# Chunked retention with a GELU layer on one core: rows of q, k, v in 1 MB loads and transposes by DMA

## The chip, the cores and the metric

The kernel runs on one core of a Trainium2 chip. A core has a matrix engine (PE), a vector engine (DVE), an activation engine (ACT), a general engine (POOL) and a queue engine (SP) that only issues transfers; ACT and POOL issue transfers too. Each engine works through its own list in order and waits on semaphores. Sixteen DMA engines move the data. The metric is the device time of one execution, in microseconds.

## The reference

Two stages. The first is a retention recurrence over 768 steps, for 4 batches and 8 heads of 64; the second is a two-layer network with GELU over the 3072 rows that come out.

```python
# q, k, v: (4, 8, 768, 64)
gamma = 1.0 - 2.0 ** (-5.0 - np.arange(H))
for t in range(S):
    state = gamma[None, :, None, None] * state + einsum('bhd,bhe->bhde', k[:, :, t], v[:, :, t])
    y[:, :, t] = 1 / sqrt(64) * einsum('bhd,bhde->bhe', q[:, :, t], state)
x = y.transpose(0, 2, 1, 3).reshape(B * S, H * D)          # (3072, 512)
h = x @ w_in                                                # (3072, 2048)
g = 0.5 * h * (1.0 + tanh(c * (h + 0.044715 * h ** 3)))
return g @ w_out                                            # (3072, 512)
```

## The kernel before

The 768 steps are cut into six chunks (c = 0 to 5) of 128 steps, and inside a chunk the recurrence is written as products. For each batch b: A = k q^T within the chunk, masked with the decay (mm_A on PE, ev_A on DVE); y = state q + A v (mm_yc and mm_yi on PE, ev_Y); and the new state from k^T v (mm_s, ev_S). Then the network runs over the 512 rows of the chunk (4 batches of 128): moe1, 16 units of four matmuls of 512 columns, each with a GELU on ACT (two units with 256 columns in moe1_two for chunks 0 and 1), and the second product. For chunks 1 to 5 the second product is made in units_w by a scheme of seven products for a 2x2 block product in place of eight: seven groups of two units, eight matmuls of 256 columns a unit, whose left operands are sums of g that g_sums makes on POOL (DVE in the last chunk), 16 instructions in a chunk.

The order of work is written out by hand. `run(units, after)` goes through a list of units and puts other work behind a numbered unit: `8: [(load, 3)]` means behind the ninth. So the attention of chunk c + 1 and the loads and casts for chunk c + 2 lie between the units of the network for chunk c. For c = 2 to 5 units 0 to 15 are moe1 and 16 to 29 units_w.

q, k and v come as f32 with 64 elements (256 bytes) in a run. For PE they are cast to f16; A needs q and k transposed, heads in pairs: 128 partitions (two heads of 64) by 128 steps, four pairs to a batch, in the tile qkT. Before the change there are two ways to it:

- By PE (chunks 0, 1, and k of chunk 2): load1 (L100) brings a batch as rows, prep1 (L184) casts it, mm_T (L222) makes four transposes on PE for each of q and k into a PSUM bank, ev_T (L234) copies that to qkT.
- By blocks (q of chunks 2 to 5, k of chunks 3 to 5): load_blk (L106) makes 16 transfers of 64 KB, each of 512 runs of 128 bytes, which lay the 32x32 blocks at the right place; prep_blk (L201) casts a batch; one DVE transpose of 32x32 blocks (L238) for a batch ends it. The state needs k as rows too, so for chunks 3 to 5 k is loaded a second time as rows and cast by a prep1 of its own.

The kernel's buffers: k and v as rows have eight slots of one batch each; q has two tiles of a chunk each; the PSUM pool has two banks "h", two "o", four "att". The transfers of q, k, v from chunk 1 on are issued by SP, which also stores a few outputs; the stores of units_w go through POOL. A transfer takes one of eight semaphores in turn and waits for the transfer before it on the same one.

Lines that the change and the prediction touch: load (L117), prep1 (L184, cast at L180 and L182 by copy_on, multiplication at L193), mm_T (L222 to L232), ev_T (L234 to L245), moe1 and its GELU (L414, L416), g_sums (L476), units_w (L518) with its copies on ACT (L559, L565) and stores on POOL (L569), the schedule for chunk 1 (L734 to L769) and the loop over chunks 2 to 5 (L772 to L803).

Of the kernel before, what the change touches and what calls it, by code (L numbers as in the profile page):

```python
# [9 lines left out]
F16 = mybir.dt.float16  # L10
F32 = mybir.dt.float32
# [5 lines left out]
def kernel(  # L17
# [9 lines left out]
    nc = tc.nc  # L27
    B, H, S, Dh = q.shape
    C = 128
    NCk = S // C  # L30
    NHP = H // 2
# [26 lines left out]
    ld = ctx.enter_context(tc.tile_pool(name="ld", bufs=2 * B))  # L58
    pre = ctx.enter_context(tc.tile_pool(name="pre", bufs=2 * B))
    att = ctx.enter_context(tc.tile_pool(name="att", bufs=4))  # L60
# [13 lines left out]
    raw = {}  # L74
    srcs = {"q": q, "k": k, "v": v}

    BLK = {"q": (2, 3, 4, 5), "k": (3, 4, 5)}

    def ld_all(key):
        if key not in raw:
            raw[key] = ld.tile(
                [128, B * NHP, 4, 32],
                F32,
                tag=key[0],
                bufs=2 if key[0] == "q32" else 1,
                name=key[0],
            )
        return raw[key]  # L90

    def ld_tile(nm, c, b):
        if nm == "q":
            t = ld_all(("q32", c)).rearrange("p (b hp) a d -> p b (hp a d)", b=B)
            return t[:, b].rearrange("p (h d) -> p h d", h=H)
        if (nm, c, b) not in raw:
            raw[nm, c, b] = ld.tile([128, H, Dh], F32, tag=f"{nm}32", bufs=8, name=f"{nm}32")
        return raw[nm, c, b]

    def load1(eng, nm, c, b):  # L100
        eng.dma_start(  # L101
            out=ld_tile(nm, c, b),
            in_=srcs[nm][b, :, c * C:(c + 1) * C, :].rearrange("h p d -> p h d"),
        )

    def load_blk(nm, c):  # L106
        t = ld_all((nm + ("32" if nm == "q" else "T32"), c))
        src = srcs[nm].rearrange("b (hp j) s (dd d) -> j dd s (b hp) d", j=2, dd=2)
        for j in range(2):
            for dd in range(2):  # L110
                for a in range(4):
                    p0, t0 = (2 * j + dd) * 32, c * C + a * 32
                    nc.sync.dma_start(  # L113
                        out=t[p0:p0 + 32, :, a, :], in_=src[j, dd, t0:t0 + 32]
                    )

    def load(c):  # L117
        load_blk("q", c)
        if c in BLK["k"]:
            for b in range(B):  # L120
                load1(nc.sync, "v", c, b)
            load_blk("k", c)
            for b in range(B):
                load1(nc.sync, "k", c, b)
        else:
            for b in range(B):
                for nm in "kv":
                    load1(nc.sync, nm, c, b)

    def hold(nm, c, b, until):  # L130

# [18 lines left out]
        out=misc[:, 0:1], in_=zero[:, 0:1], func=AF.Gelu_apprx_tanh, scale=1.0  # L150
# [14 lines left out]
    for j in range(2):  # L165
        for hp in range(NHP):
            nc.vector.tensor_scalar(
                out=mask[:, j, hp],
# [4 lines left out]
            )  # L173

    h16 = {}
    blk16 = {}

    def copy_on(eng, out, in_):
        if eng is nc.scalar:
            eng.copy(out=out, in_=in_)  # L180
        else:
            eng.tensor_copy(out=out, in_=in_)  # L182
# [15 lines left out]
            )  # L198
        h16[nm, c, b] = t

    def prep_blk(eng, nm, c, b):  # L201
        key, tag = ("q32", "q16") if nm == "q" else ("kT32", "kT16")
        t = pre.tile([128, NHP * 4, 32], F16, tag=tag, bufs=6 if nm == "q" else B, name=tag)
        copy_on(
            eng, t, ld_all((key, c))[:, b * NHP:(b + 1) * NHP].rearrange("p hp a d -> p (hp a) d")
        )
        blk16[nm, c, b] = t

    def pair(t, hp):
        return t[:, 2 * hp:2 * hp + 2]  # L210

    qkT = {}
    a_sb = {}
    xT = {}
    pss = {}
# [3 lines left out]
    def bank(tag, dt=F32, shape=(128, NHP, 128), name="ps"):  # L219
        return psum.tile(list(shape), dt, tag=tag, bufs=BANKS[tag], name=name)  # L220

    def mm_T(c, b):  # L222
        parts = [(i, nm) for i, nm in enumerate("qk") if c not in BLK[nm]]
        if not parts:
            return
        ps = bank("att", F16, (128, 2, NHP, 128), "qkT_ps")
        for i, nm in parts:
            for hp in range(NHP):
                nc.tensor.transpose(  # L229
                    out=ps[:, i, hp], in_=pair(h16[nm, c, b], hp), identity=iden  # L230
                )
        pss["T", c, b] = ps  # L232

    def ev_T(c, b, eng=nc.vector):  # L234
        t = att.tile([128, 2, NHP, 128], F16, tag="qkT", name="qkT")
        for i, nm in enumerate("qk"):
            if c in BLK[nm]:
                nc.vector.transpose(  # L238
                    out=t[:, i].rearrange("p hp t -> p (hp t)"),
                    in_=blk16.pop((nm, c, b)).rearrange("p ha d -> p (ha d)"),  # L240
                )
        if ("T", c, b) in pss:
            i0 = sum(c in BLK[nm] for nm in "qk")
            copy_on(eng, t[:, i0:], pss.pop(("T", c, b))[:, i0:])
        qkT[c, b] = t  # L245

    def mm_A(c, b):
        t = qkT[c, b]
# [90 lines left out]
    def att_T(c, *bs):  # L339
        for b in bs:  # L340
            mm_T(c, b)
            ev_T(c, b)
# [73 lines left out]
    def moe1(c, fc):  # L416
        h_ps = bank("h", shape=(128, B * C), name="h_ps")
        moe1_mm(c, fc, h_ps, 0, B * C)
        gelu(g_tile(c, fc)[:, fc % 2], h_ps)
# [177 lines left out]
    def run(units, after):  # L597
        for i, u in enumerate(units):
            u()
            for f, *args in after.get(i, ()):  # L600
                f(*args)

    VE, AC, PO, SY = nc.vector, nc.scalar, nc.gpsimd, nc.sync
# [7 lines left out]
    prep1(PO, "k", 0, 0)  # L611
    prep1(AC, "v", 0, 0)
    mm_T(0, 0)
    ev_T(0, 0, AC)
    load1(AC, "k", 0, 3)
    prep1(VE, "q", 0, 1)
    prep1(PO, "k", 0, 1)
    spin(3)
    mm_A(0, 0)
    ev_A(0, 0)  # L620
    mm_T(0, 1)
    ev_T(0, 1, AC)
    prep1(AC, "v", 0, 1)
    spin(2)
# [73 lines left out]
    def preps(c, b):  # L698
# [44 lines left out]
            4: [(att_AY, 1, (3,), "o", 1, (), VE)],  # L743
            6: [(att_S, 1, 3)],
            7: [(g_sums, PO, 1, 4, 8, 0, 1)],
            8: [(prep_blk, AC, "q", 2, 0), (load, 3)],
            9: [(prep1, AC, "k", 2, 0)],
            10: [(att_T, 2, 0), (prep_blk, AC, "q", 2, 1)],
            11: [(prep1, AC, "k", 2, 1), (g_sums, PO, 1, 0, 4, 1, 2)],
            12: [(att_T, 2, 1)],  # L750
            14: [(att_AY, 1, (), "o", 2, (0, 1), None), (prep1, PO, "v", 2, 0), (prep1, PO, "v", 2, 1)],
            15: [(g_sums, PO, 1, 4, 8, 1, 2), (prep1, PO, "v", 2, 2), (prep1, PO, "v", 2, 3)],
        },
# [1 line left out]
    run(  # L755
        units_w(1),
        {
            0: [(prep_blk, AC, "q", 2, 2), (prep1, AC, "k", 2, 2)],
            1: [(att_T, 2, 2), (prep_blk, AC, "q", 2, 3), (prep1, AC, "k", 2, 3)],
            2: [(att_T, 2, 3)],  # L760
            4: [(att_AY, 2, (0, 1), "h", 2, (2, 3), AC)],
            7: [(att_S, 2, 0, 1)],
            9: [(att_AY, 2, (2, 3), "h", 2, (), AC), (att_S, 2, 2, 3)],
            10: [(prep_blk, AC, "q", 3, 0)] + [(prep1, PO, "v", 3, b) for b in range(B)],
            11: [(prep_blk, AC, "q", 3, 1)],
            12: [(prep_blk, AC, "q", 3, 2)],
            13: [(prep_blk, AC, "q", 3, 3)],
        },
    )  # L769

# [1 line left out]
    for c in range(2, NCk):  # L772
        n, m = c + 1, c + 2
        after = {} if n == NCk else {
            12: [(att_AY, n, (), "att", n, (0, 1), None)],
            15: [(att_T, n, 3)],
            16: [(prep1, AC, "k", n, 0), (prep1, AC, "k", n, 1)],
            17: [(prep1, AC, "k", n, 2), (prep1, AC, "k", n, 3)],
            19: [(att_AY, n, (0, 1), "h", n, (2, 3), VE)],
            22: [(att_S, n, 0, 1)],  # L780
            25: [(att_AY, n, (2, 3), "h", n, (), AC), (att_S, n, 2, 3)],
        }

        def more(at, *what):
            after[at] = after.get(at, []) + list(what)

        if n < NCk:
            for b in range(B - 1):
                if c == 2:
                    more((8, 9, 11)[b], (prep_blk, AC, "k", n, b))  # L790
                more(((9, 10, 13) if c == 2 else (6, 8, 13))[b], (att_T, n, b))
            if c == 2:
                more(13, (prep_blk, AC, "k", n, 3))
        for i in range(4):
            at = 4 * i + 3
            after[at] = [(g_sums, PO if n < NCk else VE, c, 2 * i, 2 * i + 2)] + after.get(at, [])
        if m < NCk:
            more(0, (load, m))
            for b in range(B):
                more((20, 21, 23, 24)[b], (prep_blk, AC, "q", m, b))  # L800
                more(24, (prep1, PO, "v", m, b))
                more(29, (prep_blk, PO, "k", m, b))
        run([(lambda fc=fc: moe1(c, fc)) for fc in range(NF)] + units_w(c), after)  # L803


# [28 lines left out]
```

## Time and profile before

| What | Value |
|---|---|
| Device time, median of three runs | 212.72 us |
| The runs | 211.48, 212.72, 212.92 us |
| Span of the profiled execution (its own device time is not listed apart) | 209.7 us |
| PE busy | 200.6 us |
| POOL busy | 115.4 us |
| Transfers on SP's queue (q1) | 108272 packets, 21.09 MB |
| Load of q, k, v: median from issue to landing | 4.0 to 4.7 us for 256 KB on SP, 2.7 and 2.8 us for 64 KB |

The span runs from the first to the last instruction of one profiled execution, and the device time holds some microseconds around it. A line of the profile names an engine, a line of the kernel, an operation, and the tile written and read with their shapes; busy time of matmuls is modelled and can overlap. The chain of waits is followed back from the last instruction: each piece is the work that the next one waited for. SPq, ACTq and POOLq are the transfers issued by those engines.

### The profile page before, as it was taken

How to read it: one execution, taken by the hardware profiler on the slowest of the kernel's cores; microseconds unless marked ns; L12 is line 12 of the kernel's file. 1: busy time of each engine (PE TensorE's matmuls, PEld its weight loads, DVE VectorE, ACT ScalarE, POOL GpSimd, SP SyncE). 2: the span in 40 equal slices, each digit the busy share in tenths (PEclk: the TensorE clock that was granted, in tenths of full speed). 3: DMA queues.
4: the chain of work that ended last, by engine and by line, in shares of the span. 5: the costliest groups of instructions: out<-in, count | busy, mean ns of one | idle time of the engine just before them, and what ended most of it. 6: DMA issues, size and time to landing. Idle time of an engine off the chain costs nothing.

```text
span 209.7 us, 4776 instructions
## 1 busy us (share of the span) xinstructions
PE 200.6 (96%) x1928; PEld 132.0 (63%) x1928; DVE 104.1 (50%) x213; ACT 101.9 (49%) x182; POOL 115.4 (55%) x120
## 2 busy tenths in 40 slices
PE   7789999999998999999999999999999999999992
PEld 3347644456786878844688744678644788545881
DVE  4445153478734649703857630867432784053430
ACT  2474563144458615168745266643365811566311
POOL 0596001133099999249998299997499980200000
PEclk9999999999999999999999999999999999999999
DMA  7999999998899798799798698796970000500004
GB/s 168 287 253 207 206 205 222 273 269 215 157 220 233 110 179 163 110 313 177 124 219 128 124 340 131 125 207 99 206 251 0 0 3 0 203 0 0 0 28 177
DMA packets 124438, 33.19 MB, mean 158 GB/s; under 512 B 117952, under 2 KB 122432, under 8 KB 124416
## 3 DMA queue, kind: packets, MB, share of 16 engines
q1 hardware_dynamic: 108272, 21.09, 50.3%
q0 software_dynamic: 5456, 8.65, 17.4%
q10 hardware_dynamic: 10688, 3.15, 6.4%
q8 instruction: 15, 0.25, 0.4%
q14 instruction: 7, 0.06, 0.1%
HBM read 30.78 MB, written 6.29 MB: 177 GB/s over the span
## 4 chain that ended last, share of the span: by engine, by line
PE 81%; SPq 6%; ACT 4%; DMA 4%; DVE 2%; issue 1%; ACTq 1%; DVEq 0%
PE h_ps L398 35%; PE o_ps L536 29%; SPq L113 5%; PE o_ps L432 5%; PE a_ps L252 3%; PE y_ps L289 3%; PE y_ps L276 2%; DMA iden<-rr_ident 2%; DMA v<-in_v_dram 2%; PE qkT_ps L229 2%; PE spin_ps L156 1%; SPq L101 1%; PE s_ps L313 1%; ACT g L414 1%; ACTq L101 1%
## 5 line engine op out<-in xcount | busy, mean ns | idle before, releaser
L398 PE MATMUL h_ps<-xT,w_in 128*128 128x512 f16 (+2 forms) x488 | 87.4, 334 | 0.5 <-ACT g L414 0.5
L414 ACT ACTIVATE g<-h_ps 128x512 f16<-128x512 f32 (+1 forms) x98 | 57.5, 589 | 33.9 <-PE h_ps L398 33.5
L398 PEld LDWEIGHTS <-w_in 128*128 128x128 f16 x488 | 45.3, 97 | 37.4 <-issue 2.8
L467 POOL TENSOR_TENSOR s_g<-g 128x512 f16<-128x512 f16 x32 | 36.9, 1152 | 9.4 <-ACT g L414 9.4
L265 DVE TENSOR_TENSOR a_sb<-a_ps,mask 128x512 f16<-128x512 f32 x48 | 30.1, 682 | 23.1 <-PE a_ps L252 23.1
L536 PEld LDWEIGHTS <-s_g 128*128 128x128 f16 x320 | 30.2, 98 | 4.3
L536 PE MATMUL o_ps<-t_w,s_g 128*128 128x256 f16 x240 | 27.8, 273 | 0.0
L536 PEld LDWEIGHTS <-g 128*128 128x128 f16 x240 | 23.4, 98 | 3.6
L467 POOL TENSOR_TENSOR s_g<-s_g,g 128x512 f16<-128x512 f16 x16 | 18.4, 1153 | 1.3
L536 PE MATMUL o_ps<-w_out,g 128*128 128x256 f16 x160 | 18.6, 273 | 0.0
L467 POOL TENSOR_TENSOR s_g<-g,s_g 128x512 f16<-128x512 f16 x16 | 18.5, 1153 | 0.0
L193 POOL TENSOR_TENSOR k<-k,cst 128x512 f16<-128x512 f32 x8 | 8.3, 1044 | 17.3 <-DMA k<-in_k_dram 17.3
L569 POOL DMA_DIRECT2D out_dram<-o_sb x8 | 5.9, 737 | 20.3 <-DVE o_sb L467 16.8
L193 POOL TENSOR_TENSOR v<-v,cst 128x512 f16<-128x512 f32 x16 | 16.2, 1044 | 0.0
L238 DVE STREAM_TRANSPOSE qkT<-kT 128x512 f16<-128x512 f16 x12 | 8.1, 678 | 15.0 <-ACT kT L180 9.5
L565 ACT COPY o_sb<-o_ps 128x512 f32<-128x512 f32 (+1 forms) x5 | 2.7, 543 | 25.1 <-PE o_ps L536 25.1
L432 PE MATMUL o_ps<-w_out,g 128*128 128x512 f16 x64 | 14.8, 380 | 0.0
L305 DVE TENSOR_TENSOR xT<-y_ps,dec 128x512 f16<-128x512 f32 x16 | 10.3, 686 | 4.5 <-PE y_ps L289 4.5
L238 DVE STREAM_TRANSPOSE qkT<-q 128x512 f16<-128x512 f16 x16 | 11.0, 690 | 2.6 <-ACT q L180 2.5
L559 ACT COPY s_u<-o_ps 128x512 f32<-128x512 f32 (+1 forms) x6 | 3.1, 514 | 17.6 <-issue 9.9
L330 DVE SCALAR_TENSOR_TENSOR st<-st,cst,s_ps 128x128 f16<-128x128 f16 (+1 forms) x40 | 10.1, 313 | 2.0 <-PE s_ps L313 2.0
L156 PE MATMUL spin_ps<-zero 128*128 128x512 f16 x32 | 9.4, 429 | 1.2 <-DVE zero L148 1.2
(55 smaller groups left out, 185.3 us busy)
## 6 DMA issues: line engine op xcount, KB each, us to landing
k<-in_k_dram SPq DMA_DIRECT2D x22, 256.0 KB, 4.7
v<-in_v_dram SPq DMA_DIRECT2D x18, 256.0 KB, 4.0
q<-in_q_dram SPq DMA_DIRECT2D x64, 64.0 KB, 2.8
out_dram<-o_sb POOLq DMA_DIRECT2D x8, 512.0 KB, 5.2
kT<-in_k_dram SPq DMA_DIRECT2D x48, 64.0 KB, 2.7
w_in<-in_moe_w_in_dram POOLq DMA_DIRECT2D x4, 512.0 KB, 9.3
w_out<-in_moe_w_out_dram POOLq DMA_DIRECT2D x4, 512.0 KB, 14.7
v<-in_v_dram ACTq DMA_DIRECT2D x6, 256.0 KB, 5.5
```

The lines of the kernel that those rows point to most:

```text
L113: nc.sync.dma_start(out=t[p0:p0 + 32, :, a, :], in_=src[j, dd, t0:t0 + 32])
L156: nc.tensor.matmul(out=ps, lhsT=zero[:, 0:128], rhs=zero, start=True, stop=True)
L193: eng.tensor_tensor(out=t, in0=src, in1=cst[:, col:col + H].unsqueeze(2).broadcast_to([128, H, Dh]), op=ALU.mult,)
L238: nc.vector.transpose(out=t[:, i].rearrange("p hp t -> p (hp t)"), in_=blk16.pop((nm, c, b)).rearrange("p ha d -> p (ha d)"),)
L265: nc.vector.tensor_tensor(out=s, in0=ps[j], in1=mask[:, j], op=ALU.mult)
L305: nc.vector.tensor_tensor(out=x, in0=ps, in1=dec, op=ALU.mult)
L330: nc.vector.scalar_tensor_tensor(out=t[:, :, hp], in0=t[:, :, hp], scalar=cst[:, OG + hp:OG + hp + 1], in1=s_ps[:, :, hp], op0=ALU.mult, o ...
L398: nc.tensor.matmul(out=out, lhsT=w_in_sb[wi][:, kc, wr * 128:(wr + 1) * 128], rhs=xT[c][:, kc, t0:t1], start=(kc == 0), stop=(kc == NHP - ...
L414: nc.scalar.activation(out=out, in_=in_, func=AF.Gelu_apprx_tanh, scale=1.0)
L432: nc.tensor.matmul(out=ps[:, n0:n1], lhsT=g_sb[c, fc // 8][:, fc % 8, b * C:(b + 1) * C], rhs=w_out_sb[fc // (NF // NO)][:, fc % (NF // NO ...
L467: eng.tensor_tensor(out=out, in0=in0, in1=in1, op=op)
L536: nc.tensor.matmul(out=po, lhsT=lhs(c, lk, fp, a), rhs=rhs(rk, fp), start=(new and fp == 0 and (last or a == 0)), stop=(stop and fp == NP ...
```

## The change

For chunks 2 to 5 q, k and v are each loaded by one transfer of 1 MB (128 steps on the partitions, 32 batch-heads of 64) into tiles of a whole chunk, two slots each; this replaces 16 block transfers for q, the same for k from chunk 3, and four transfers by batch for v and for k as rows. k is loaded once and cast once. q and k, cast to f16, are transposed by a DMA from SBUF to SBUF, issued by SP, one for each of q and k of a batch: 32 in all. The casts move in the schedule with them, and the load of chunk 3 moves from behind unit 8 of chunk 1's first product to behind unit 1 of its second. Chunks 0 and 1 keep PE's transposes.

```diff
+    def raw_of(nm, c):
+        if (nm, c) not in raw:
+            raw[nm, c] = ld.tile([128, B * H, Dh], F32, tag=f"{nm}32", bufs=2, name=f"{nm}32")
+        return raw[nm, c]
...
     def load(c):
-        load_blk("q", c)
-        if c in BLK["k"]:
-            for b in range(B):
-                load1(nc.sync, "v", c, b)
-            load_blk("k", c)
-            for b in range(B):
-                load1(nc.sync, "k", c, b)
-        else:
-            for b in range(B):
-                for nm in "kv":
-                    load1(nc.sync, nm, c, b)
+        for nm in "qkv":
+            nc.sync.dma_start(
+                out=raw_of(nm, c),
+                in_=srcs[nm][:, :, c * C:(c + 1) * C, :].rearrange("b h p d -> p (b h) d"),
+            )
...
+    def dma_T(nm, c, *bs):
+        for b in bs:
+            nc.sync.dma_start_transpose(
+                out=qkT_of(c, b)[:, "qk".index(nm)],
+                in_=h16[nm, c, b].rearrange("p h d -> p (h d)"),
+            )
...
-            8: [(prep_blk, AC, "q", 2, 0), (load, 3)],
-            9: [(prep1, AC, "k", 2, 0)],
-            10: [(att_T, 2, 0), (prep_blk, AC, "q", 2, 1)],
-            11: [(prep1, AC, "k", 2, 1), (g_sums, PO, 1, 0, 4, 1, 2)],
-            12: [(att_T, 2, 1)],
+            8: [(prep1, AC, "q", 2, 0), (prep1, AC, "k", 2, 0), (dma_T, "q", 2, 0), (dma_T, "k", 2, 0)],
+            9: [(prep1, AC, "q", 2, 1), (prep1, AC, "k", 2, 1), (dma_T, "q", 2, 1), (dma_T, "k", 2, 1)],
+            11: [(g_sums, PO, 1, 0, 4, 1, 2)],
...
-            0: [(prep_blk, AC, "q", 2, 2), (prep1, AC, "k", 2, 2)],
-            1: [(att_T, 2, 2), (prep_blk, AC, "q", 2, 3), (prep1, AC, "k", 2, 3)],
-            2: [(att_T, 2, 3)],
+            0: [(prep1, AC, "q", 2, 2), (prep1, AC, "k", 2, 2), (dma_T, "q", 2, 2), (dma_T, "k", 2, 2)],
+            1: [(prep1, AC, "q", 2, 3), (prep1, AC, "k", 2, 3), (dma_T, "q", 2, 3), (dma_T, "k", 2, 3), (load, 3)],
...
-            10: [(prep_blk, AC, "q", 3, 0)] + [(prep1, PO, "v", 3, b) for b in range(B)],
-            11: [(prep_blk, AC, "q", 3, 1)],
-            12: [(prep_blk, AC, "q", 3, 2)],
-            13: [(prep_blk, AC, "q", 3, 3)],
+            10: [(prep1, AC, "q", 3, 0)] + [(prep1, PO, "v", 3, b) for b in range(B)],
+            11: [(prep1, AC, "q", 3, 1), (prep1, AC, "k", 3, 0)],
+            12: [(prep1, AC, "q", 3, 2), (prep1, AC, "k", 3, 1)],
+            13: [(prep1, AC, "q", 3, 3), (prep1, AC, "k", 3, 2), (prep1, AC, "k", 3, 3), (dma_T, "q", 3, 0, 1, 2, 3), (dma_T, "k", 3, 0, 1, 2, 3)],
...
         if m < NCk:
             more(0, (load, m))
             for b in range(B):
-                more((20, 21, 23, 24)[b], (prep_blk, AC, "q", m, b))
+                more((20, 21, 23, 24)[b], (prep1, AC, "q", m, b))
                 more(24, (prep1, PO, "v", m, b))
-                more(29, (prep_blk, PO, "k", m, b))
+                more(29, (prep1, PO, "k", m, b))
+            more(29, (dma_T, "q", m, *range(B)), (dma_T, "k", m, *range(B)))
```

In the loop the entries that called att_T and made the second cast of k (behind units 6 to 13 and 15 to 17) are taken out.

## The prediction

> **What bounds the kernel now.** I read the page first: the span, the busy shares and the slices.
>
> ```profile
> span 209.7 us, 4776 instructions
> PE 200.6 (96%) x1928; PEld 132.0 (63%) x1928; DVE 104.1 (50%) x213; ACT 101.9 (49%) x182; POOL 115.4 (55%) x120
> PE   7789999999998999999999999999999999999992
> PEclk9999999999999999999999999999999999999999
> ```
>
> PE is idle for 9.1 us in all, mostly in the first slices, and its granted clock is full. So the change can gain only PE instructions or PE waits. The view of PE's waits says what is left:
>
> ```profile
> PE qkT_ps L229 <- ACT k L180: 1.3, 3, 0.5
> PE spin_ps L156 <- DVE zero L148: 1.2, 1, 1.2
> ```
>
> No wait names DVE's transposes (L238). The chain of waits, read in order of time, shows where the sets of chunk 2 lie, and that from 74.39 us to the tail at 205.7 only PE stands on the path:
>
> ```profile
> 64.74 0.05 issue
> 64.79 0.40 PE qkT_ps L229 x4
> ...
> 73.82 0.53 ACT k L180
> 74.35 0.05 issue
> 74.39 0.40 PE qkT_ps L229 x4
> ...
> 88.15 11.69 PE h_ps L398 x52
> 99.84 0.55 PE a_ps L252 x16
> ```
>
> Last, the queues. The page's DMA issues give size and median time to landing:
>
> ```profile
> q<-in_q_dram SPq DMA_DIRECT2D x64, 64.0 KB, 2.8
> v<-in_v_dram SPq DMA_DIRECT2D x18, 256.0 KB, 4.0
> out_dram<-o_sb SPq DMA_DIRECT2D x2, 128.0 KB, 1.7
> ```
>
> The timelines of ACT and POOL (start, duration, engine, line, operation) place the casts and sums that the change moves or delays:
>
> ```profile
> 62.63 0.60 ACT L414 ACTIVATE g<-h_ps 128x512 f16<-128x512 f32 x1 [0.28 <-PE h_ps L398]
> 63.12 0.61 ACT L180 CAST q<-q 128x512 f16<-128x512 f32 x1
> ...
> 92.45 1.14 POOL L467 TENSOR_TENSOR s_g<-g 128x512 f16<-128x512 f16 x1 [2.65 <-ACT g L414]
> ...
> 107.38 1.15 POOL L467 TENSOR_TENSOR s_g<-s_g,g 128x512 f16<-128x512 f16 x1
> ```
>
> **Removed, at no gain.** 28 DVE transposes (L238, 11.0 + 8.1 us) and 12 casts of k on ACT (0.51 us apart, 6.1 us) go. From 88 us on PE runs beside them without a wait, so they are worth nothing there. The second load of k and the 112 block transfers go too; no wait of PE names a load after the identity's at the start.
>
> **Removed, on the path: chunk 2.** PE loses 16 transposes, four to a set, 0.23 us a set (42.41 to 42.64 us), and waits for k's cast. Around the first two sets PE's stream halts 0.86 us (64.16 to 65.02) and 0.72 us (66.77 to 67.49). After the change ACT makes two casts behind each of the gelus of units 8 and 9. At its spacing of 0.50 to 0.51 us: gelu 8 at 62.63, casts 63.12 and 63.63, gelu 9 at 64.14, casts 64.65 and 65.16, gelu 10 at 65.67. There are two h banks, so unit 11 waits for gelu 9 (64.78 instead of 64.16) and unit 12 for gelu 10 (66.31 instead of 65.65): 1.28 us lost in place of 1.58. The product of q and k for batch 0 (L252) comes 0.3 us earlier, at 69.0, for batch 1 at 69.3. For batches 2 and 3 another 0.23 and 0.87 us go (72.65 to 72.88, 73.76 to 74.63): their products could start at 75.9 and 76.2.
>
> **Added: 32 transposing transfers.** The program has one instruction for each q or k of a batch, 128x512 f16 (128 KB) in 32 tiles of 16 rows by 128 columns. The trace has none. Two prices matter: p, from one to the next on SP's queue, and the time to landing. Low end of p: 512 runs of 256 B are read, and the block loads, with 512 runs too, are issued 0.49 us apart where nothing holds them. High end: a tile is written as 128 runs of 32 B, 4096 a transfer; the page's q1 row makes 0.503 x 209.7 us x 16 / 108272 packets = 15.6 ns a packet and engine, so 4096 / 16 x 15.6 ns = 4.0 us. I take 1.0, the pitch of the 256 KB loads (0.85 to 1.14 us, 1024 runs each), between both sides and nearest to them in bytes. Landing: 1.7 us (128 KB store) to 4.0 (256 KB load); I take 2.8, the 64 KB row with as many runs.
>
> Batches 0 and 1: casts end at 63.7, 64.3, 65.3, 65.8; transfers issue at 63.8, 64.8, 65.8, 66.8; the last lands at 69.6, product wanted at 69.3: 0.3 us, the gain is gone. Batches 2 and 3: casts end at 72.1, 72.6, 73.8, 74.3; issues at 72.1, 73.1, 74.1, 75.1; the last lands at 77.9, where the product of batch 3 was at 77.3 before: +0.6.
>
> The Trainium skill has two rules that disagree here, and no run before this one can decide. Its page VectorE: DVE Perf Modes, in The three transpose paths, gives 1309 ns for a 128x128 transpose by DMA against 390 ns on TensorE; four in series would be 5.2 us (an estimate from that page) and a sum beyond the slow rival's below. Its page Advanced Engine Details and Errata, in X-Bar Transpose (TRN2), calls such transfers as fast as regular ones, 350 to 400 GB/s; that is 0.35 us for 128 KB (an estimate), less than an issue, and the sum would be the quick rival's.
>
> **Moved: the load of chunk 3.** SP is in order. The load goes from behind unit 8 of chunk 1's first product (64.86 us) to behind all eight transfers of chunk 2, 76.1 us, as three transfers of 1 MB. One queue moved 268 GB/s of such short rows (62 to 64 us; with two queues 288): 11.7 us. Fixed part 2.0 us, between the 1.7 of the store and 2.7 less 0.24 of the block loads. q lands near 82, k near 86, v at 89.8. Two users:
>
> - ACT casts k of batches 2 and 3 after the last output copy (88.19) and ahead of gelu 0 of chunk 2 (89.19). Two casts more, 1.0 us, and PE's third unit waits for that gelu (two banks): +1.0 on PE, so +1.6 with the 0.6.
> - POOL casts v only when the whole 1 MB is there: 89.8 + 4.05 (four casts, from 110.72) = 93.9, then two store issues that stand behind them, 0.75 and 0.73, to 95.4; then the sums, which began at 92.45. They run back to back to 111.9. The last slice of the second sum ended at 108.53 where PE takes it at 108.20 + 6 x 0.109 = 108.85: 0.3 us of slack. POOL is 2.95 late, so PE stands at +2.65 from there. This is the later of the two.
>
> **Elsewhere.** At the start ACT's issue of v of batch 2 now waits for the first v (1.23 + 4.9 = 6.13 us) and not for the identity (5.96): +0.15, on the chain. Chunk 3: its transfers end by about 95, wanted at 99.8. Chunk 4: POOL casts k from 120.72 to 123.0, k of batch 1 lands by 126, wanted at 130.7; chunk 5 the same, 30.6 us later. Nothing at p = 1; with p = 2 the last k of a pair comes at 127, still hidden.
>
> **Sum.** 2.65 + 0.15 = +2.8 on a span of 209.7, 212.5. Around the span lie 212.72 - 209.7 = 3.0 us (against the median of three runs, 211.48 to 212.92; the profiled execution's own time is not listed): 215.5.
>
> **Rivals.**
>
> *Quick transfers (not slower).* p = 0.49. For: the issue row of the block loads, and the DMA engines are empty of loads when chunk 2's transfers run. Then the products of batches 0 and 1 keep their 0.3, the last transfer issues at 74.05, load 3 at 74.55, POOL's sums start at 93.85, +1.4 less 0.3, with the start +1.25: 214.0; at 288 GB/s 213.2. It is under 1% up to p of about 0.8, which gives +2.1. Against: a tile's writes are eight times shorter than any row of a load.
>
> *A slow crossbar.* p = 4.0, landing 6.0. Batch 1's product waits until 81.8 (+12.2), batch 3's until 102.3 (+25.0), load 3 issues at 100.3 and POOL stands at +26.9. Then each chunk's eight transfers take 32 us, more than the 30.6 us of a chunk, and k comes after all q: some 10 to 12 us more in each of chunks 3, 4 and 5, near 274. For: the packet arithmetic. Against: 32 x 4 us would be 128 us of all sixteen engines.
>
> *A gain.* Transfers land in 1.7 us, v reaches POOL by 86 (it must, for its sums to start at 92), and the 1.0 us on ACT falls in PE's slack: -0.3 - 1.1, 211.3. The load would need over 330 GB/s, which no stretch of such rows shows.
>
> *p of 1.83*, the longest single issue in the trace (ACT's queue, 2.90 us, held by full rings): batch 1 at 72.1 (+2.5), load 3 at 81.9, POOL +8.45: 221.3. It is the upper end of the forecast.
>
> **Numbers.** Forecast (p from 0.8 to 1.83): 0.50, 215.5, own range 214.9 to 221.3. Quick: 0.36. Slow crossbar: 0.07, with 0.03 for p between. Gain: 0.04. Range 212.8 to 221.3: it leaves out the slow side, the gain and a sliver of the quick case, under 2 in 10. Under 1% can't be told from no change here (the three runs span 0.7%); 1% is 2.1 us. Faster 0.04, same 0.37, slower 0.59.
>
> **What would show it.** The page's DMA issues would give p and landing; the profile after has no L229 in chunk 2 and no STREAM_TRANSPOSE. PE's waits should name a DMA into qkT for L252 near 69 and 77, gelu's L414 line near 90 us, and POOL's s_g for L536 near 108. POOL should wait for v of chunk 3 until about 90. I am wrong if PE waits in chunks 3 to 5 (p above 2), if SP issues load 3 before 75 (p below 0.8), or if POOL's sums begin before 93.

## The result, and the profile after

The changed kernel is slower: 220.09 us (median of four runs, 218.76 to 221.82) against 212.82 us for the kernel before in the same comparison (211.48 to 213.56). The ratio is 1.0341, with an interval from 1.0267 to 1.0415. The profiled run took 221.32 us, of which 219.5 are its span. Medians here and below are of all runs, but ratios compare only the runs within 1.5% of the fastest of their kernel, so a ratio can differ from that of the two medians.

The page after, the same four lines as before:

```profile
span 219.5 us, 4596 instructions
...
PE 203.0 (92%) x1912; PEld 133.2 (61%) x1912; DVE 85.0 (39%) x181; ACT 96.4 (44%) x170; POOL 115.5 (53%) x120
...
PE   7889999999996969889957999999999999999993
...
PEclk9999999999999999999995899999999999999999
```

PE does 16 instructions fewer and is busy 2.4 us longer; it is idle for 16.5 us instead of 9.1. With 5.49 us a slice the dents in its digits lie between 66 and 121 us, and the granted clock is down at the last of them. Before the change PE's row had an 8 there, at 63 to 68 us, where PE waited for k's casts, and the clock's row nothing. The view of PE's waits (total, number of times, longest) names three:

```profile
PE a_ps L214 <- DMA qkT<-k: 3.9, 2, 2.2
PE o_ps L498 <- POOL s_g L429: 3.8, 1, 3.8
PE h_ps L360 <- ACT g L376: 2.9, 5, 1.5
```

L214 is the product of q and k, L498 the second product of the network, L360 the first; before the change they had the numbers 252, 536 and 398. All three are waits that the prediction asked the reader to look for. Where they stand is shown by PE's timeline (start, duration, line, operation, and in brackets the idle time before it and who ended it):

```profile
71.10 0.40 PE L214 MATMUL a_ps<-qkT 64*128 64x128 f16 x8 [1.67 <-DMA qkT<-k]
...
79.92 0.40 PE L214 MATMUL a_ps<-qkT 64*128 64x128 f16 x8 [2.18 <-DMA qkT<-k]
...
94.00 9.72 PE L360 MATMUL h_ps<-xT,w_in 128*128 128x512 f16 x44 [1.45 <-ACT g L376]
...
112.08 0.83 PE L498 MATMUL o_ps<-t_w,s_g 128*128 128x256 f16 x6
116.69 4.02 PE L498 MATMUL o_ps<-t_w,s_g 128*128 128x256 f16 x18 [3.78 <-POOL s_g L429]
...
124.56 0.63 PE L238 MATMUL y_ps<-qkT,st 64*64 64x128 f16 x16
```

Before the change the last of these groups, and the y behind it, were:

```profile
108.20 2.79 PE L536 MATMUL o_ps<-t_w,s_g 128*128 128x256 f16 x24
...
114.02 0.64 PE L276 MATMUL y_ps<-qkT,st 64*64 64x128 f16 x16
```

The 24 instructions that are cut in two at 116.69 ran in one piece of 2.79 us before. Here the last 18 alone take 4.02 us, where 18/24 of 2.79 would be 2.1 us: that is the clock.

Why qkT is late, and why POOL is late behind it, stands in the timeline of SP's queue (start, time that the issue took):

```profile
63.76 1.31 SPq L204 DMA_TRANSPOSE qkT<-q  x1
65.17 1.21 SPq L204 DMA_TRANSPOSE qkT<-k  x1
66.48 1.21 SPq L204 DMA_TRANSPOSE qkT<-q  x1
67.78 2.10 SPq L204 DMA_TRANSPOSE qkT<-k  x1
73.65 1.19 SPq L204 DMA_TRANSPOSE qkT<-q  x1
...
77.55 1.22 SPq L204 DMA_TRANSPOSE qkT<-k  x1
79.23 0.71 SPq L95 DMA_DIRECT2D q<-in_q_dram  x1
80.40 3.26 SPq L95 DMA_DIRECT2D k<-in_k_dram  x1
84.11 3.96 SPq L95 DMA_DIRECT2D v<-in_v_dram  x1
```

Within a set of four, one transposing transfer follows the other after 1.28 to 1.41 us (1.30 in the median). The load of chunk 3 comes behind the eighth, at 79.23; before the change SP had issued it from 64.86 us on:

```profile
64.86 9.84 SPq L113 DMA_DIRECT2D q<-in_q_dram  x16
```

The chain of waits (start, duration, engine) carries the lateness on, from the load to PE:

```profile
80.40 9.28 DMA k<-in_k_dram
...
94.00 1.04 PE h_ps L360 x4
95.04 0.02 issue
95.06 0.11 POOL v L162
...
99.10 1.42 POOL out_dram L531 x2
100.53 0.02 issue
100.55 1.16 POOL s_g L429
...
116.69 4.02 PE o_ps L498 x18
```

From 116.69 to the tail it is PE alone again. The view puts PE's first product ahead of POOL's casts of v at 95.06, but that is its inference from the event nearest in time; POOL had stood idle for 14.89 us, and the view of the tile v between 78 and 100 us gives this load of 1 MB 10.8 us from issue to landing, which is 94.9 us:

```profile
L95 SPq DMA_DIRECT2D v<-in_v_dram x1: 3955/3955/3955, 84.1 to 84.1; - x1
...
DMA to landing us min/median/max: 10.8/10.8/10.8
```

So POOL waited for v. One experiment below moves these casts and takes PE's wait away.

The same instruction in both timelines shows where the time is lost:

| Row of PE | before, start | after, start | later by |
|---|---|---|---|
| first product of chunk 2 begins (x52 / x8) | 87.99 | 90.66 | 2.67 |
| second product, s_g group that is cut above | 108.20 | 112.08 | 3.88 |
| its next piece, with the wait of 3.78 | | 116.69 | 7.66 (3.88 + 3.78) |
| y of chunk 3 behind it | 114.02 | 124.56 | 10.54 |
| last group of the kernel | 203.78 | 214.32 | 10.54 |
| end of the span | 209.7 | 219.5 | 9.8 |

So 3.88 us come from qkT and the GELU, 3.78 from POOL's sums, 2.88 between there and 124.56 without any wait, and then, through all of chunks 3 to 5, nothing: their 24 transposing transfers and the loads of chunks 4 and 5 lie wholly beside PE's work. (The tail gives 0.7 back.) The 2.88 are clock. The view by stretches has the columns start:end, length, busy time and count of PE, PEld, DVE, ACT, POOL, the granted clock, the DMA share and GB/s:

```profile
114.00:116.00 2.00, 0.00 (x0) 0.00 (x0) 1.65 (x3) 0.00 (x0) 1.92 (x3) 0.92 1.06 333
116.00:118.00 2.00, 1.31 (x7) 0.94 (x8) 0.00 (x0) 0.00 (x0) 2.00 (x3) 0.50 0.87 159
118.00:120.00 2.00, 2.00 (x11) 1.45 (x10) 0.00 (x0) 0.91 (x2) 2.00 (x3) 0.50 0.00 0
120.00:122.00 2.00, 2.00 (x24) 1.26 (x23) 0.67 (x3) 0.19 (x1) 2.00 (x3) 0.50 0.28 65
122.00:124.00 2.00, 2.00 (x18) 1.68 (x16) 0.45 (x2) 1.03 (x3) 0.85 (x1) 0.87 0.01 0
```

Summing what is missing to 1.00, half clock held for 0.32 + 3 x 2.00 + 0.52 = 6.8 us, of which the first part fell into the wait. How long it holds differs from run to run, and the time with it: the four runs had a mean clock of 0.992, 0.992, 0.984 and 0.977 and took 218.76, 218.87, 221.32 and 221.82 us. The two profiled runs (9.8 us apart in span) are thus the shortest of before and the second longest of after; the medians differ by 7.3.

### The profile page after: what moved, and what is told of

Its sections match the earlier page's. It is cut to its first block, busy times and chain, and to the rows that moved or that the text cites. A ratio compares the mean times of both kernels' runs of the same rounds, so it can differ in the third digit from the quotient of the medians.

```text
span 219.5 us, 4596 instructions
## 1 busy us (share of the span) xinstructions
PE 203.0 (92%) x1912; PEld 133.2 (61%) x1912; DVE 85.0 (39%) x181; ACT 96.4 (44%) x170; POOL 115.5 (53%) x120
## 4 chain that ended last, share of the span: by engine, by line
PE 71%; POOL 17%; DMA 4%; ACT 4%; issue 2%; DVE 1%; SPq 0%; POOLq 0%; ACTq 0%
PE h_ps L360 29%; PE o_ps L498 22%; POOL s_g L429 13%; PE o_ps L394 6%; DMA k<-in_k_dram 4%; PE spin_ps L126 4%; POOL v L162 3%; PE y_ps L251 2%; PE a_ps L214 2%; PE y_ps L238 2%; PE qkT_ps L187 1%; PE s_ps L275 1%; ACT g L376 1%; ACT qkT L149 1%; POOL out_dram L531 1%
## 5 line engine op out<-in xcount | busy, mean ns | idle before, releaser
L360 PE MATMUL h_ps<-xT,w_in 128*128 128x512 f16 (+2 forms) x488 | 87.1, 334 | 2.9 <-ACT g L376 2.9
L360 PEld LDWEIGHTS <-w_in 128*128 128x128 f16 x488 | 45.5, 98 | 39.7 <-issue 5.0
L498 PEld LDWEIGHTS <-s_g 128*128 128x128 f16 x320 | 31.4, 102 | 9.4 <-POOL s_g L429 4.1
L498 PE MATMUL o_ps<-t_w,s_g 128*128 128x256 f16 x240 | 30.4, 288 | 3.8 <-POOL s_g L429 3.8
L498 PEld LDWEIGHTS <-g 128*128 128x128 f16 x240 | 23.5, 98 | 3.6
L498 PE MATMUL o_ps<-w_out,g 128*128 128x256 f16 x160 | 18.3, 273 | 0.0
L214 PE MATMUL a_ps<-qkT 64*128 64x128 f16 x192 | 8.5, 218 | 4.3 <-DMA qkT<-k 3.9
L126 PE MATMUL spin_ps<-zero 128*128 128x512 f16 x32 | 10.7, 478 | 1.2 <-DVE zero L118 1.2
L214 PEld LDWEIGHTS <-qkT 64*128 64x128 f16 x192 | 5.4, 94 | 8.4 <-DMA qkT<-k 4.2
```

What stands on the lines that cost most here:

```text
L126: nc.tensor.matmul(out=ps, lhsT=zero[:, 0:128], rhs=zero, start=True, stop=True)
L214: nc.tensor.matmul(out=ps[j][:, hp], lhsT=t[j * 64:(j + 1) * 64, 1, hp], rhs=t[j * 64:(j + 1) * 64, 0, hp], start=True, stop=True,)
L360: nc.tensor.matmul(out=out, lhsT=w_in_sb[wi][:, kc, wr * 128:(wr + 1) * 128], rhs=xT[c][:, kc, t0:t1], start=(kc == 0), stop=(kc == NHP - ...
L498: nc.tensor.matmul(out=po, lhsT=lhs(c, lk, fp, a), rhs=rhs(rk, fp), start=(new and fp == 0 and (last or a == 0)), stop=(stop and fp == NP ...
```

## The experiments

The theory after the result: (1) the price of a transposing transfer is one of issue on SP's queue, 1.3 us each; (2) it delays qkT, and by the load behind it also v of chunk 3, POOL's sums and PE; (3) the idle gaps cost a second time by the clock. Rivals: that the 1 MB loads themselves or the transfers of chunks 3 to 5 cost time; that the price goes by tiles or bytes; that the clock drops by chance.

**Chunk 2 back to PE's transposes** (e1 in the expectations below), q's too, which had gone by blocks before the change: PE makes 16 transposes more than there. The 1 MB loads and the 24 transfers of chunks 3 to 5 stay.

```diff
-            8: [(prep1, AC, "q", 2, 0), (prep1, AC, "k", 2, 0), (dma_T, "q", 2, 0), (dma_T, "k", 2, 0)],
+            8: [(prep1, AC, "q", 2, 0), (load, 3)],
+            9: [(prep1, AC, "k", 2, 0)],
+            10: [(att_T, 2, 0), (prep1, AC, "q", 2, 1)],
...
```

> Chunk 2 goes back to PE's transposes and the load of chunk 3 back behind unit 8 of chunk 1; the 1 MB loads and the 24 transposing transfers of chunks 3 to 5 stay. Theory A (the loss comes from the place of eight transfers and of one load in SP's queue): PE waits for no transfer into qkT, POOL has v of chunk 3 before 87 us and its sums start as before, only the two casts of k ahead of chunk 2's first GELU stay (+1.0 us): span 210 to 211.5, the time 0 to 0.8% above before. Theory B (transposes and 1 MB loads cost wherever they stand, by contention in the DMA engines): at least half of the 7.3 us stays, 216 us or more, with PE or POOL waits in chunks 3 to 5.

Measured: 211.77 us against 213.31, ratio 0.9972 (0.9939 to 1.0004): no difference from the kernel before that can be told. PE's waits:

```profile
PE h_ps L360 <- ACT g L376: 1.5, 3, 1.0
...
PE qkT_ps L187 <- ACT k L149: 0.2, 1, 0.2
```

No wait for qkT's transfers, none for s_g. So the whole loss sits in chunk 2's eight transfers and in the load that stood behind them; the rest of the change is no loss. The 1.0 us on the GELU that the prediction worked out for the two added casts is there by itself. The wait for k's cast in chunk 2, 1.3 us before the change, is down to 0.2, with q's transposes ahead of k's; the time came out just under the 0 to 0.8% above that was expected.

**k of chunk 3 cast ahead of the last output copy** (e8), on top of the kernel just told (the casts behind units 10 to 13 move up one place, the transfers stay behind 13).

> As e1 (chunk 2 on PE), with the casts of k of chunk 3 ahead of the last output copy of chunk 1. The one PE wait that e1 had more than before (1.0 us on the first GELUs of chunk 2) goes: span near 208.8, 0.3 to 0.7% below before. If that wait was covered by something else, no change from e1 (0.3% below before, with an interval that reaches none).

Measured: 210.77 us against 211.79, ratio 0.9952 (0.9926 to 0.9979). The longest GELU wait goes from 1.0 to 0.2 us (0.5 us in all, as before the change). Against the kernel before that is 0.3 to 0.7% less, as expected. Its time can't be told from that of the kernel without the move by these two intervals; the profile shows the wait gone, but its span is 210.0 us, since PE waits 1.4 us at the start for the network's first weights in this run.

**v of chunk 3 off POOL** (e2). Its casts go to DVE, behind unit 5 of chunk 2; the queue of SP stays as it is.

```diff
-            10: [(prep1, AC, "q", 3, 0)] + [(prep1, PO, "v", 3, b) for b in range(B)],
+            10: [(prep1, AC, "q", 3, 0)],
...
+        if c == 2:
+            for b in range(B):
+                more(5, (prep1, VE, "v", n, b))
```

> As the changed kernel, but DVE and not POOL casts v of chunk 3, behind unit 5 of chunk 2. Theory A: v still lands near 95 us, but POOL starts its sums near 94 and PE's stall of 3.8 us on s_g goes, and with it the stretch at half the granted clock behind it; the waits on chunk 2's transfers (3.9 us) and on the GELU (2.9 us) stay: span about 213.5, 1.5 to 2.2% above before. Theory A' (the late v costs little; the transfers' waits alone carry the loss): within 1 us of the changed kernel, 219 us or more.

Measured: 217.82 us against 213.31, ratio 1.0165 (1.0047 to 1.0283, from its two shortest runs), runs from 214.87 to 219.53. The wait for s_g is gone from the list, and the two for qkT stay (4.2 us): POOL was late through v, and not through the stores or the sums. The interval is wide because the runs differ in their clock: 1.0 in that of 214.87 us, 0.982 in those of 217.37 and 219.53. In the profiled run (218.27 us, clock 0.992) it drops in another place, after the second qkT wait. PE's timeline:

```profile
73.42 0.40 PE L214 MATMUL a_ps<-qkT 64*128 64x128 f16 x8 [2.04 <-DMA qkT<-k]
...
82.24 0.40 PE L214 MATMUL a_ps<-qkT 64*128 64x128 f16 x8 [2.19 <-DMA qkT<-k]
...
83.14 4.46 PE L498 MATMUL o_ps<-t_w,s_g 128*128 128x256 f16 x24
```

The same 24 matmuls took 2.79 us at this place in the changed kernel. This run also waited 1.5 us for the first weights at the start; without that and the 1.7 us of clock its span of 216.4 us is near the 213.5 that was expected. The one run that kept its clock at 1.0 throughout, 214.87 us, agrees with the table above: without the 3.78 and the 2.88, 211.48 + 3.88 - 0.7 = 214.7.

**Work for PE during the wait for s_g** (e5). 14 matmuls on zeros behind unit 19 of chunk 2, nothing else.

```diff
+        if c == 2:
+            more(19, (spin, 14))
```

> As the changed kernel, with 14 matmuls on zeros (0.216 us each, 3.0 us) where PE stands idle for POOL's sums of chunk 2; they end before the sums do and change no result. If the idle stretch is what halves the granted clock behind it, the clock stays full from 112 to 124 us, the 7 us at half clock go, and the span falls by 2 to 2.5 us to about 217, 2% above before, though PE has more to do. If the clock falls for another reason, the span stays at 219 or more.

Measured: 218.91 us against 211.79, ratio 1.031 (1.026 to 1.036). Three runs had a clock of 1.0 and the fourth 0.992, where all four of the changed kernel were below 1.0. The profiled one is the 0.992; it has its drop at 81 to 84.5 us, behind the second wait for qkT, and none behind the sums:

```profile
113.77 3.18 PE L126 MATMUL spin_ps<-zero 128*128 128x512 f16 x14 [0.56 <-DVE xT L267]
116.79 2.78 PE L498 MATMUL o_ps<-t_w,s_g 128*128 128x256 f16 x24
```

The group resumed at 116.69 in the changed kernel; here it starts at 116.79, with all 24 still ahead, and runs at full speed; the y of chunk 3 comes at 122.60 in place of 124.56. So the drop behind the sums comes from the gap there, and it cost the profiled run some 2 us. The drop behind the second wait for qkT (2.19 us here) is missing in the changed kernel's profile, behind the same wait of 2.18 us: whether a gap of that length costs the clock varies from run to run. In the medians (1.2 us, from two comparisons whose intervals overlap) the gain isn't established. The three runs at full clock took 218.65 to 218.94 us, and two runs of the changed kernel at 0.992 took 218.76 and 218.87, so what the clock costs a typical run stays open.

**One transfer for q and k of a batch** (e3): 64 tiles instead of 32, half as many instructions.

```diff
-        for b in bs:
+        for b in bs if nm == "k" else ():
...
-                out=qkT_of(c, b)[:, "qk".index(nm)],
-                in_=h16[nm, c, b].rearrange("p h d -> p (h d)"),
+                out=qkT_of(c, b).rearrange("p i hp t -> p (i hp) t"),
+                in_=qk16[c, b].rearrange("p i h d -> p (i h d)"),
```

> As the changed kernel, but q and k of a batch lie in one tile and go in one transposing transfer of 64 tiles: 16 instructions for 32. If SP's 1.2 us is the price of an instruction, one takes 1.2 to 1.3 us still, chunk 2's last lands near 76, the load of chunk 3 issues near 75 and the time falls to about 2% above before. If it is the price of 32 tiles, one takes 2.4 us, the last lands near 79 and the time stays within 1% of the changed kernel.

Measured: 217.71 us against 213.31, ratio 1.0247 (1.0177 to 1.0316). The view of one line's instructions, for L204 of the changed kernel (issue time in ns, shortest, median, longest):

```profile
L204 SPq DMA_TRANSPOSE qkT<-k x16: 1207/1218/2443, 65.2 to 166.4; - x16
...
DMA to landing us min/median/max: 2.3/2.4/7.3
```

and for the same call, now L208, with the joint transfers:

```profile
L208 SPq DMA_TRANSPOSE qkT<-qk x16: 1231/1234/2382, 64.6 to 162.5; - x16
...
DMA to landing us min/median/max: 2.7/2.8/5.5
```

Twice the tiles, and the issue takes 1.23 us in place of 1.22. The price is one of the instruction. The wait for qkT falls from 3.9 to 1.0 us and the load of chunk 3 moves up from 79.23 to 76.07 us; the wait for s_g stays at 3.8, since PE comes as much earlier as POOL does.

**The transfers of chunk 2 earlier** (e4): the casts spread over units 2 to 13 of chunk 1's first product, each with its transfer, and the load of chunk 3 behind unit 13. The casts of k of chunk 3 move up as in the second experiment.

```diff
+            2: [(prep1, AC, "q", 2, 0), (dma_T, "q", 2, 0)],
...
+            13: [(prep1, AC, "k", 2, 3), (dma_T, "k", 2, 3), (load, 3)],
```

> As the changed kernel, but the casts of chunk 2 stand behind units 2 to 13 of chunk 1's first product, each with its transfer behind it; the load of chunk 3 follows behind unit 13, and chunk 3's casts of k stand ahead of the last output copy. Theory A: all eight transfers have landed before PE asks (k of batch 1 by 68 us, of batch 3 by 71), v of chunk 3 lands before 87, no cast stands ahead of chunk 2's first GELU; PE is spared 16 transposes (0.9 us) and 1.2 us of waits for k's casts: span 207.5 to 208.5, 0.5 to 1.2% below before. Theory B: 216 us or more, since the same transfers and loads remain.

Measured: 213.41 us against 213.31, ratio 1.0002 (0.9956 to 1.0048): the loss is gone, but the gain that was expected isn't there. The traced run has one wait for qkT, 1.50 us. It also has one at the start, 1.3 us for the network's first weights, which stands in four of the nine profiles of these experiments (1.3 to 1.5 us) and so isn't of this edit; without the two the span of 209.7 us would be 206.9. The ten runs sort by their mean clock: two at 1.0 (211.34 and 211.48 us), five at 0.992 (212.65 to 213.82), three at 0.984 (214.06 to 215.27). So eight runs of ten lost clock in a kernel whose traced run has one new wait of 1.5 us in its middle. A step of 0.008 in the mean clock is one stretch of 3.4 us at half (3.4 x 0.5 / 212), and it goes with about 1.9 us, by the medians of the three groups. Where the clock was lost in those runs isn't traced; the traced run kept it. The wait itself has a cause in SP's queue: the first transfer's issue took 4.24 us, right behind the load of v for chunk 2, issued at 53.41.

**The load of chunk 3 first** (e7), ahead of chunk 2's transfers in SP's order.

```diff
+            8: [(load, 3), (prep1, AC, "q", 2, 0), (prep1, AC, "k", 2, 0), (dma_T, "q", 2, 0), (dma_T, "k", 2, 0)],
```

> As the changed kernel, with the load of chunk 3 ahead of chunk 2's eight transfers in SP's queue and nothing else moved. Theory A (one queue in order, one victim for another): v of chunk 3 lands near 72 and POOL is never late, but the first transfers issue some 5 us later behind the load, and PE waits 4 to 6 us for batches 0 and 1 near 70 us: 2 to 3% above before, with a wait on qkT and none on s_g. If only the late v counted, the time would be within 1% of before.

Measured: 223.65 us against 211.79, ratio 1.0551 (1.0501 to 1.06), worse than expected. The wait for s_g is gone, so it is the place behind the transfers that makes v late. But now the transfers stand behind three loads. SP's queue:

```profile
65.95 3.40 SPq L95 DMA_DIRECT2D v<-in_v_dram  x1
69.46 4.69 SPq L204 DMA_TRANSPOSE qkT<-q  x1
74.26 1.19 SPq L204 DMA_TRANSPOSE qkT<-k  x1
```

and PE, which waits for qkT three times (10.0 us in all, the third 1.66 us at 89.19):

```profile
76.64 0.61 PE L214 MATMUL a_ps<-qkT 64*128 64x128 f16 x8 [6.32 <-DMA qkT<-k]
79.26 0.61 PE L214 MATMUL a_ps<-qkT 64*128 64x128 f16 x8 [2.01 <-DMA qkT<-k]
```

The expectation had missed the 4.69 us of the first issue behind a load, and half clock for 10.2 us from 72 us on and 3.4 us more from 89.6 us on (0.61 in place of 0.40 us for the same eight instructions).

**Both together** (e6): the joint transfers (e3) and their early places (e4).

> The early casts of e4 and the joint transfers of e3 together, so SP issues four transposes for chunk 2 in place of eight. Theory A: the 1.5 us that PE waited at 71 us in e4 go (batch 1's transfer issues near 64.5 and lands by 68), load of chunk 3 issues near 70 and v lands by 85: span 207 to 208.5 (or 1.3 more where the first w_in is late, as in e4's profile), 0.5 to 1.3% below before. Theory B: no gain over e4, 0% against before.

Measured: 209.27 us against 211.79, ratio 0.9849 (0.9807 to 0.9892): faster than before. No wait names qkT's transfers. The load of chunk 3 is issued at 71.32 us, v comes to POOL at 85.94, and of the wait for s_g there is this left:

```profile
PE o_ps L502 <- POOL s_g L433: 0.9, 1, 0.9
```

**And v of chunk 3 on DVE with it** (e9).

> As e6, with v of chunk 3 cast by DVE behind unit 5 of chunk 2 and not by POOL. In e6 PE still waits 0.9 us for POOL's sums of chunk 2, which began behind v's casts. If that is the last of the late load, the wait goes and the span falls by about 0.9 us to some 206.8, 1.3 to 2.2% below before. If PE would only wait for the next thing, it stays at e6's 1.5%.

Measured: 207.93 us against 212.96, ratio 0.9773 (0.9734 to 0.9811), the best of these. The wait for s_g is 0.4 us, and PE is busy 199.5 us of a span of 206.8, the span that was expected. Whether PE's own transposes with casts as early would have come as far wasn't tried, so this gain isn't one of the DMA's transposes alone.

## Why the prediction was right in kind and short in size

**Right.** The direction and the range (220.09 in 212.8 to 221.3). The mechanism, step by step: the removed DVE transposes, casts and block transfers gained nothing; the loss is on the path of chunk 2 alone; SP's order puts the load of chunk 3 behind eight transfers; v is late at POOL, with the two store issues behind its casts, then the sums, then L498. The timing of PE's units between the casts came as worked out: unit 11 at 64.80 (forecast 64.78), unit 12 at 66.33 (66.31), the product of batch 0 at 69.04 (69.0). Chunks 3 to 5 hide the transfers, though with less room than forecast: chunk 3's were to end by about 95 us, and the last was issued at 101.36; PE, itself late, asked for them from 103.65 on.

**The term that was mis-sized: the price p.** The prediction took 1.0 us, the pitch of a 256 KB load, as nearest in bytes. It is 1.30 us, inside its range of 0.8 to 1.83, and it goes neither by bytes nor by runs or tiles, as the joint transfers show. With it went the chain that hangs on p, and further than p alone would have moved it:

| Step | forecast | measured |
|---|---|---|
| product of batch 1 (us) | 69.6 | 71.10 |
| first transfer of batch 2 | 72.1 | 73.65 |
| load of chunk 3 issued | 76.1 | 79.23 |
| v of chunk 3 at POOL | 89.8 | 95.06 |
| sums begin | 95.4 | 100.55 |
| PE's delay behind the sums | +2.65 | +7.66 |

Of the 3.1 us at the load, 1.55 are there at the first transfer of batch 2, since the casts follow a PE that the first wait had made late: 1.0 from the pitch of the transfers ahead of the fourth, and 0.5 because the fourth landed 3.3 us after its issue, where 2.8 were forecast and 2.4 is the median. Its issue took 2.10 us (1.98 in the run with matmuls on zeros) for a reason that no run shows. Another 1.2 come from the pitch of the four transfers of batches 2 and 3, and 0.4 from the 1.68 us between the last of them and the load. The other 2 us up to v are a load that took 15.8 us from its first issue to POOL's first cast, where 13.7 were forecast. Transposing transfers of chunk 3 are issued while it runs (from 88.18 us on), but so they are in the kernel with joint and early transfers (from 82.19), where the same load took 14.6 us; the cause stays open.

With p = 1.30 the prediction's own sum makes batch 1 at 70.5, the load at 78.2, POOL +4.75 and 217.6 us. The upper end of its range, 221.3, was p = 1.83, from an issue of that length at 2.90 us on ACT's queue; the row shows how long it was, and no row shows why. So it was partly luck that 220.09 lies in the range: the room that 1.83 left for p was filled by the longer load, the fourth transfer and the clock. The GELU's wait was 1.45 us, not 1.0: ACT itself waited 3.18 us for k to land.

**The term that was missing: the clock.** The prediction counted PE's waits once. 2.88 us of the 9.8 came from running at half clock behind them. No row of the kernel before had such a gap in the middle of the program, so its profile couldn't price it. The Trainium skill, TensorE: Matmul & The Clock Gate, Part 1, states that the clock is either full or half and is set by windows of 3413 ns that run freely; the stretches of 3.4, 6.8 and 10.2 us measured here are one, two and three of these. Its table Why this matters for your kernels warns of idle gaps above some 3 us; here the clock fell behind waits of 2.0 and 2.2 us, 9 us apart (e2), and behind one of 1.66 us that followed others (e7), and the measurement decides.

**Smaller slips.** One is the 3.0 us around the span. The run of 221.32 us has 1.8, and so, within 0.1, has every run that lists both; the profiled run of before, 209.7 us, must therefore be the one of 211.48. On its own time the forecast was 214.3 us, a little farther off. The +0.15 at the start left nothing: PE begins the same product at 54.81 us in both traces. The end of POOL's sums, 111.9 in the prediction, should be 113.7 (95.4 + 18.3, their length before); nothing is built on it. And the tile's writes of 32 bytes are four times shorter than the block loads' runs of 128, not eight times shorter than any row of a load.

**The rivals.** Quick transfers fall with p = 1.30, though the data itself is quick: the stretches of 0.2 us show the engines moving one transfer in 0.6 to 0.7 us, at a peak of 293 GB/s, and idle till the next. The slow crossbar falls by its packet count: the trace has 2179 packets for four transfers, 545 each, where the arithmetic took 4096. The two rows (a stretch with the columns as above, and the packets from 63.5 to 72 us):

```profile
75.00:75.20 0.20, 0.20 (x4) 0.18 (x3) 0.00 (x0) 0.20 (x1) 0.20 (x1) 1.00 1.29 293
...
DMA packets 2179, 0.54 MB, mean 64 GB/s; under 512 B 2178, under 2 KB 2178, under 8 KB 2178
```

Of the Trainium skill's two rules, the series of 1309 ns a block (VectorE: DVE Perf Modes, The three transpose paths) doesn't hold here: a transfer with four such blocks is issued in 1.21 us and lands after 2.4, and one with eight takes 1.23 and 2.8. The other (Advanced Engine Details and Errata, X-Bar Transpose (TRN2)) calls transposing transfers as fast as regular ones, which fits the data in flight (a peak of 293 GB/s, where the loads before the change made 268 to 288); its 350 to 400 GB/s are not reached, and 128 KB every 1.30 us are about 100 GB/s. It says nothing of the issue, which is what counted. The gain rival failed for this order of work, and not for the transfers: joined and issued early, they gave it.

## What to carry to other kernels

Count the instructions that a change puts on an in-order queue, give each a price by the instruction and not by its bytes, and ask first what stands behind them: here the load for the next chunk cost more than the data that was waited for. Where the price is by the instruction, fewer and larger ones, issued before their data is wanted, turn the same transfers from a loss of 3.4% into a gain of 1.5%. A new idle gap of some 2 us on PE is to be counted with what the clock may take after it, and a kernel whose runs scatter should be sorted by granted clock before its median is explained. Not all scatter is clock, though: in one comparison 17 runs of the kernel before went from 211.35 to 213.42 us, all at 0.996 or more.

## What the runs showed of the hardware

- A transposing transfer within SBUF occupies SP's queue for 1.21 us with 32 tiles (128 KB) and 1.23 us with 64 (256 KB), with 1.30 us from one to the next in chunk 2; it lands 2.4 and 2.8 us after its issue in the median, and the DMA engines work on 128 KB for only 0.6 to 0.7 us of that.
- Close behind a 1 MB load of 256-byte runs on the same queue, the first such issue takes 4.0 to 4.7 us instead of 1.2 (the changed kernel at 88.18 us, e4, e5, e7). Where it was issued 2.2 to 3.0 us after the load's issue had ended, it took 2.0 to 2.8 (e3, e6, e9), and 5.1 us after it 1.31: where it was held, it came to its end 4.5 to 5.2 us after the end of the load's issue. Why isn't shown.
- The clock falls to half during or behind waits that were 1.7 to 6.3 us long, not each time (the profiled run of the changed kernel kept it after waits of 1.67 and 2.18 us), for 3.4, 6.8 or 10.2 us; 14 matmuls on zeros in the gap of 3.8 us kept it up there.
